# A two-branch attention kernel: another order of the first two groups, K of the first heads through two PSUM banks, and polynomial exponentials from group 1 on

## The chip, the cores and the metric

One Trainium2 chip, one core. The metric is device time in microseconds of one launch, the median of several runs. The engines named below are TensorE (PE, with its weight loads as PEld), VectorE (DVE), ScalarE (ACT), GpSimd (POOL) and SyncE (SP), which issues the DMAs.

## The reference

The input x has 2048 tokens of 640 features. Two attention branches with 32 heads of 20 features each are computed from the same x with weights of their own, and mixed by a gate for every token:

```python
qkv = (x @ wqkv).reshape(B, S, 3, 32, 20)
# A: full softmax attention over all 2048 keys
p = softmax(einsum("bhqd,bhkd->bhqk", q, k) * 20**-0.5);  a = (p @ v) @ wo
# B: each position attends to itself and 7 earlier ones, 2 apart
logits = einsum("bhsd,bhswd->bhsw", q, kg) * 20**-0.5;    b = (softmax(logits) @ vg) @ wo
g = sigmoid((x * gate_w).sum(-1))
out = g * a + (1 - g) * b
```

Branch A is by far the larger part: 32 heads x 2048 x 2048 exponentials.

## The kernel before, in words

**Tiling.** The heads of branch A are taken four at a time: `q` counts the eight quads of heads. One quad lies on the 128 partitions in four strips of 32, of which 21 are used (20 features, and one row that carries a shift, so that no maximum over the scores is needed). The queries are cut into four chunks `qc` of 512. A *group* is one quad with one query chunk, so there are 32 groups, numbered `g = qc * 8 + q`: all quads of the first chunk, then all of the second. A group has 16 key blocks of 128 keys times 4 heads = 64 *units*. One unit is a QK matmul of 128 keys x 512 queries, an exponential of 128 x 512, and a PV matmul.

**The main stream.** Units are gathered into *tiles* that use two PSUM areas in turn: `score[0]` with three banks (1536 columns) and `score[1]` with two (1024). For each tile, `qk` (L1090) issues its QK matmuls, `exp` (L1107) one ScalarE instruction over the whole tile into one of six `ebuf`s, and, two or more tiles later, `pv` (L1137) accumulates into the one bank `obank`. When a group's last PV is done, `close` adds `gen_norm`, which normalises and transposes the output into a slot of `oTn` on VectorE (L544 to L558).

**VectorE units ("rides").** In tiles of `score[0]` the third unit can be given to VectorE: the tile's exponential is then 1024 wide, and `gen_d` computes the third by a polynomial, in one step out of PSUM (L1101) and three more (L570, L573, L576). `wanted` decides where, once the planner's clock has passed `D0`, if VectorE is free enough. Whatever a VectorE unit does not take, ScalarE does.

**Everything else** runs beside that stream as generators with a priority number (the smaller, the sooner): `gen_k(q)` and `gen_q(g)` project K of a quad and Q of a group through one of the two `side` banks (the matmuls of all generators are recorded at L444), `gen_v(half)` projects V for four quads, `gen_gate` makes the gate of a chunk, `gen_bweights` reorders the weights of branch B on GpSimd (L590), `gen_bproj` and `gen_b` compute branch B, `gen_fold` and `gen_prefold` apply the output projections, and `tail` finishes the last chunk. A planner with costs of its own decides, at the time the program is written out, how these are interleaved in each engine's fixed order; TensorE runs strictly in that order. If the queries of the next group are not ready when its first tile comes, `run_until` puts all that is missing into the order at once. TensorE's gaps are filled with matmuls that compute nothing (`filler`, L1151 and L1155).

A new group starts its projections when the group ahead of it begins:

```python
if g1 + 1 < NQ:
    add_gen(gen_k(g1 + 1), 2)
add_gen(gen_q(g1 + 1), 2)
```

so each of the first eight groups needs a new K (four token chunks, 20 matmuls) as well as a Q.

**The start.** `turned(tcc)` transposes 512 tokens of x on TensorE into both score areas, ScalarE copies three fifths of the result (L917) and VectorE two fifths (L920). `k_first(tcc)` projects K of quad 0 for these tokens into `side[0]`; VectorE takes the largest magnitude of each row (L934), and after that ScalarE copies K to `kT` (L937). All four `tcc` use the same bank. `v_first` projects the first two V blocks, and Q of group 0 goes through `side[1]`.

Of the kernel before, what the change touches and what calls it, by code (L numbers as in the profile page):

```python
# [14 lines left out]
P = 128  # L15
# [3 lines left out]
DH = 20  # L19
# [10 lines left out]
TOK = 256  # L30

# [209 lines left out]
def _build(ctx, nc, A_x, A_wqkv, A_wo, B_wqkv, B_wo, gate_w, out):  # L241
# [114 lines left out]
    T("dve", 0.1, lambda e: e.memset(zero[:, :], 0.0), writes=["zero"])  # L356

    for i in range(7):
        T("pe", 0.43, lambda e: e.matmul(obank[:, :], qabs[:, 0:P], qabs[:, :], start=True, stop=True), reads=["qabs"], writes=["obank"])
# [120 lines left out]
    def gen_q(g):  # L480
        qc, q = divmod(g, NQ)
# [38 lines left out]
    def gen_gate(qc):  # L520
        while qc > 1 and not all(done.get(("norm", (qc - 2) * NQ + q)) for q in range(NQ)):
            yield ("cond",)
# [18 lines left out]
    def gen_norm(g):  # L541
        qc, q = divmod(g, NQ)
        sl = g % NSLOT
# [204 lines left out]
    def gen_prefold():  # L748
        while not (done.get(("b", 2 * QCN - 1)) and all(done.get(("norm", LQ + q)) for q in range(NQ - 1))):
            yield ("cond",)  # L750
# [61 lines left out]
    def gen_fold(qc):  # L812
        while not (done.get(("b", 2 * qc + 1)) and all(done.get(("norm", qc * NQ + q)) for q in range(NQ))):
            yield ("cond",)
# [99 lines left out]
    def turned(tcc):  # L914
        cols = slice(tcc * 512, (tcc + 1) * 512)
        turn(tcc, 0, 3, 0)
        T("act", actc(1536), lambda e: e.activation(  # L917
            xT[:, 0:3, cols], _ap(score[0], 0, [[512, 3], [1, 512]]), ACTF.Copy), reads=[("score", 0)], writes=[("xT", tcc, 0)])
        turn(tcc, 3, 5, 1)
        T("dve", dvc(1024), lambda e: e.tensor_copy(xT[:, 3:5, cols], _ap(score[1], 0, [[512, 2], [1, 512]])),  # L920
          reads=[("score", 1)], writes=[("xT", tcc, 1)])
# [7 lines left out]

    def k_first(tcc):  # L930
        cols = slice(tcc * 512, (tcc + 1) * 512)
        T("pe", 1.07, proj5(side[0][:, :], lambda c: kvw[:, WKP_OFF + c * NQ * P:WKP_OFF + c * NQ * P + P], None, tcc * 512),
          reads=[("WkP", 0)] + XT(tcc), writes=[("side", 0)])
        T("dve", dvc(512), lambda e: e.tensor_reduce(  # L934
            kmx4[:, tcc:tcc + 1], side[0][:, :], AX.X, ALU.max, apply_absolute_value=True),
          reads=[("side", 0)], writes=[("kmx4", tcc)])
        T("act", actc(512), lambda e: e.activation(kT[:, 0, cols], side[0][:, :], ACTF.Identity, bias=onesrow[:, 0:1]),  # L937
          reads=[("side", 0), "onesrow", ("kmx4", tcc)], writes=[("kT", 0, tcc)])

    def v_first(kb0, n, s_):  # L940
# [6 lines left out]
        T("pe", 0.67 * n, fn, reads=["WvA"] + XT(kb0 // 4) + XT((kb0 + n - 1) // 4), writes=[("score", s_)])  # L947
        for i in range(n):
            o = _ap(vA, (kb0 + i) * NQ * 4 * DV + 1, [[DV, 16], [1, DH]])
            i_ = _ap(score[s_], i * 512, [[DH, 16], [1, DH]])  # L950
            T("act", actc(320) + 0.1, lambda e, o=o, i_=i_: e.activation(o, i_, ACTF.Copy), reads=[("score", s_), "vAones"],
              writes=[("vA", kb0 + i, 0)])
            done[("v", kb0 + i, 0)] = True

    turned(0)
    T("dve", 0.36, w_pad(kvw, WKP_OFF, repB[0], 0, 4 * DH, 0), reads=["wk0", "WkP"], writes=[("WkP", 0)])
    T("dve", 0.36, w_pad(WqP, 0, repB[1], 0, 4 * DH, 0), reads=["wq0", "WqP"], writes=[("WqP", 0)])
    done[("pad", 0)] = True
    turned(1)
    k_first(0)  # L960
    T("pe", 1.07, proj5(side[1][:, :], lambda c: WqP[:, c, 0:P], None, 0), reads=[("WqP", 0)] + XT(0), writes=[("side", 1)])
    turned(2)
# [3 lines left out]
    k_first(1)  # L966
    turned(3)
    k_first(2)
    T("dve", 0.5, lambda e: e.memset(vA[:, :, :, :, 0:1], 1.0), writes=["vAones"])
    k_first(3)  # L970
    T("dve", 0.15, lambda e: e.tensor_reduce(kmx[:, 0:1], kmx4[:, :], AX.X, ALU.max),
# [3 lines left out]
    v_first(0, 2, 1)  # L975
    T("pe", 0.215, lambda e: e.matmul(side[1][:, :], KM[0][:, :], qabs[:, :], start=False, stop=True, skip_group_check=True),
      reads=[("KM", 0), "qabs"], accum=[("side", 1)])
    t = T("dve", dvc(512), lambda e: e.tensor_scalar(qT[0][:, :], side[1][:, :], OCT, offs[:, 0:1], op0=ALU.mult, op1=ALU.add),
# [21 lines left out]

    DTIME = 15.0
    DIDLE = -1.0
    D0 = 100.0
# [73 lines left out]
    def qk(s):  # L1077
# [8 lines left out]
        def fn(e):  # L1086
            ins = None
            for g, kb, j, o in lst:
                q = g % NQ
# [5 lines left out]
        for g, kb, j, _ in lst:  # L1095
            rd.add(("kT", g % NQ, kb // 4))
            rd.add(("qT", g % 2))
# [13 lines left out]
    def pv(units, quads):  # L1111
# [14 lines left out]
        for g, kb, j, _ in lst:  # L1126
            if not done.get(("v", kb, (g % NQ) // 4)):
                run_until(("v", kb, (g % NQ) // 4))
            rd.add(("vA", kb, (g % NQ) // 4))
# [4 lines left out]
        def fn(e):  # L1134
            ins = None
            for k, (g, kb, j, src) in enumerate(lst):
                ins = e.matmul(obank[32 * j:32 * j + DV, :], vA[:, kb, g % NQ, j, :], src,  # L1137
# [24 lines left out]
    def close(g):  # L1162
        nonlocal hold, obank_free
        if g >= NSLOT:
            run_until(("fold", (g - NSLOT) // NQ))
# [7 lines left out]
    obank_free = 0.0  # L1173
# [34 lines left out]
    while pvg < NG:  # L1208
# [11 lines left out]
        if acting:  # L1220
            gn = us[-1] // 64
            run_until(("q", gn))
            if gn != g1:
                g1 = gn

                if g1 + 1 < NG:
                    if g1 + 1 < NQ:
                        add_gen(gen_k(g1 + 1), 2)
                    add_gen(gen_q(g1 + 1), 2)
                if g1 == 1:  # L1230
                    add_gen(gen_v(1), 3)
                if g1 == 0:
                    add_gen(gen_gate(0), 3)
                if g1 == 2:
                    add_gen(gen_bweights(), 4)
                if g1 % NQ == 6 and g1 // NQ + 1 < QCN:
# [55 lines left out]
```

## Time and profile before

| | |
|---|---|
| time, three runs | 944.18, 946.05, 944.18 us; median 944.18 us |
| profiled run | 943.52 us, span of the profile 941.7 us, mean granted TensorE clock 0.992 |
| PE busy | 913.5 us, 97%, fillers included |
| ACT busy | 907.7 us, 96% |
| DVE busy | 684.1 us, 73% |
| POOL busy | 23.7 us, 3% |
| exponentials L1107 | 819 instructions, 891.7 us |

The span is one execution, from its first to its last instruction. A row of the timeline gives start and length of one instruction, or of several like ones that follow each other; the number of instructions is behind the x. The bracket at its end is the time that the engine stood idle ahead of it, and the instruction whose end released it. "Busy" of successive ScalarE instructions overlaps a little, so 819 exponentials at their mean length add up to more than the time that they fill.

### The profile page before, as it was taken

What the parts mean: (1) busy time and instruction counts of PE and PEld (TensorE: products, weight loads), DVE (VectorE), ACT (ScalarE), POOL (GpSimd) and SP (SyncE); (2) the same over time, 40 slices, a digit from 0 to 9 for tenths busy, and PEclk for the clock granted to TensorE, in tenths of its full rate; (3) what the DMA queues carried; (4) which work ended last, traced back from release to release, by engine and by line L of the source; (5) the groups of instructions that cost most, each with busy time, mean ns of one, the idle gap of its engine ahead of it and who ended that gap; (6) DMA issues with size and microseconds to landing.
All of it is one profiled execution on the core that took longest, in us unless ns stands there. A gap on an engine that the chain in (4) does not pass through costs nothing.

```text
span 941.7 us, 16802 instructions
## 1 busy us (share of the span) xinstructions
PE 913.5 (97%) x6827; PEld 313.6 (33%) x6827; DVE 684.1 (73%) x1174; ACT 907.7 (96%) x854; POOL 23.7 (3%) x20
## 2 busy tenths in 40 slices
PE   7989999998999999999999999999999999999997
PEld 4323322222333333333333333333433333343223
DVE  5655587778688878777687887688788565778872
ACT  5979999997999999999999999999999999999996
POOL 0000000009000000000000000000000000000000
PEclk9999999998999999999999999999999999999999
DMA  7110000020000000000000000000000000000000
GB/s 225 27 44 1 1 1 1 1 106 1 1 2 1 1 2 1 8 15 8 1 1 2 1 1 8 15 9 1 1 1 1 9 8 16 1 1 1 1 1 29
DMA packets 9769, 13.08 MB, mean 14 GB/s; under 512 B 2396, under 2 KB 8412, under 8 KB 9692
## 3 DMA queue, kind: packets, MB, share of 16 engines
q1 hardware_dynamic: 9692, 12.00, 3.9%
q8 instruction: 54, 0.88, 0.4%
q14 instruction: 23, 0.19, 0.1%
HBM read 9.38 MB, written 2.62 MB: 13 GB/s over the span
## 4 chain that ended last, share of the span: by engine, by line
ACT 42%; PE 41%; issue 12%; DVE 4%; DMA 0%; DVEq 0%; ACTq 0%
ACT ebuf L1107 41%; PE side L444 16%; PE score L1090 12%; PE obank L1137 7%; PE side L1151 2%; PE obank L1155 2%; DVE tD L570 1%; DVE gtan L1101 1%; PE side L926 1%; DMA oTn<-in_A_x_dram 0%; PE score L908 0%; ACT tB L694 0%; PE side L651 0%; DVE tD L573 0%; DVE eD L576 0%
## 5 line engine op out<-in xcount | busy, mean ns | idle before, releaser
L1107 ACT ACTIVATE ebuf<-score 128x1024 bf16<-128x1024 f32 (+1 forms) x819 | 891.7, 1303 | 13.6 <-PE score L1090 13.0
L1090 PE MATMUL score<-qT,kT 32*128 32x512 bf16 x2048 | 320.7, 385 | 10.3 <-ACT ebuf L1107 4.2
L1137 PE MATMUL obank<-ebuf,vA 128*21 128x512 bf16 x1953 | 179.8, 386 | 1.2 <-ACT ebuf L1107 1.2
L1090 PEld LDWEIGHTS score<-qT,kT 32*128 32x128 bf16 x2048 | 79.9, 91 | 251.7 <-ACT ebuf L1107 189.1
L444 PE MATMUL side<-xT,kvw 128*128 128x256 bf16 (+1 forms) x740 | 137.6, 297 | 0.0
L1101 DVE TENSOR_SCALAR gtan<-score 128x512 f32<-128x512 f32 x77 | 53.3, 692 | 72.0 <-PE score L1090 71.3
L1155 PE MATMUL obank<-xT,zero 128*128 128x512 bf16 x298 | 88.5, 383 | 0.0
L444 PEld LDWEIGHTS side<-xT,kvw 128*128 128x128 bf16 x740 | 58.7, 97 | 61.0 <-issue 46.6
L1137 PEld LDWEIGHTS obank<-ebuf,vA 128*21 128x21 bf16 x1953 | 41.4, 89 | 94.7 <-issue 88.4
L1151 PE MATMUL side<-xT,ident 128*128 128x512 bf16 x189 | 57.6, 384 | 0.0
L576 DVE SCALAR_TENSOR_TENSOR eD<-tD,gtan 128x512 int16<-128x512 f32 x77 | 54.4, 707 | 1.5
L570 DVE SCALAR_TENSOR_TENSOR tD<-gtan 128x512 f32<-128x512 uint16 x77 | 53.6, 696 | 2.2
L573 DVE SCALAR_TENSOR_TENSOR tD<-gtan,tD 128x512 f32<-128x512 uint16 x77 | 53.5, 694 | 1.6
L444 PE MATMUL side<-xT,WqP 128*128 128x512 bf16 x155 | 49.3, 393 | 5.3 <-DVE qB L624 4.5
L719 DVE TENSOR_TENSOR stage<-vB,repB 128x1280 bf16<-128x1280 bf16 x64 | 50.3, 821 | 1.0
L444 PE MATMUL side<-stage,ident 128*128 128x512 bf16 (+1 forms) x192 | 49.5, 348 | 0.0
L641 DVE TENSOR_TENSOR stage<-qB,kB 128x1280 bf16<-128x1280 bf16 x64 | 49.1, 820 | 0.3
L444 PE MATMUL side<-woA_r,oTn 128*128 128x512 bf16 (+1 forms) x248 | 49.3, 302 | 0.0
L1155 PEld LDWEIGHTS obank<-xT,zero 128*128 128x128 bf16 x298 | 24.0, 97 | 36.3 <-issue 25.1
L469 DVE TENSOR_SCALAR kT<-side,onesrow 128x512 bf16<-128x512 f32 x28 | 20.8, 744 | 19.8 <-PE side L444 19.5
L444 PE MATMUL side<-woBp,oB 128*128 128x512 bf16 (+1 forms) x160 | 33.3, 303 | 0.0
L544 DVE STREAM_TRANSPOSE oTt<-obank 128x512 f32<-128x512 f32 x32 | 22.8, 712 | 13.0 <-PE obank L1137 12.8
(126 smaller groups left out, 640.4 us busy)
## 6 DMA issues: line engine op xcount, KB each, us to landing
stage<-in_B_wqkv_dram SPq DMA_DIRECT2D x1, 2400.0 KB, 8.8
out_dram<-outsb SPq DMA_DIRECT2D x12, 160.0 KB, 1.8
stage<-in_A_wqkv_dram SPq DMA_DIRECT2D x1, 1600.0 KB, 11.7
oTn<-in_A_x_dram SPq DMA_DIRECT2D x2, 640.0 KB, 5.2
kvw<-in_A_wqkv_dram SPq DMA_DIRECT2D x1, 800.0 KB, 8.7
woA_r<-in_A_wo_dram SPq DMA_DIRECT2D x4, 200.0 KB
woBp<-in_B_wo_dram SPq DMA_DIRECT2D x5, 160.0 KB
oB<-in_A_x_dram SPq DMA_DIRECT2D x1, 640.0 KB, 7.0
```

Of the source, the lines that this page charges most:

```text
L444: ins = e.matmul(o, l, r, start=(first and i == 0), stop=(last and i == n - 1), skip_group_check=True)
L570: T("dve", dvc(512), lambda e: e.scalar_tensor_tensor(tD[:, :], nn, -OCT16, nn, op0=ALU.add, op1=ALU.mult), reads=[("xD", w)], writes=["tD"])
L573: T("dve", dvc(512), lambda e: e.scalar_tensor_tensor(tD[:, :], nn, H1, tD[:, :], op0=ALU.add, op1=ALU.mult), reads=[("xD", w), "tD"], wri ...
L576: T("dve", dvc(512), lambda e: e.scalar_tensor_tensor(eD[:, sl, :].bitcast(I16), tD[:, :], H2, xD[w][:, :], op0=ALU.mult, op1=ALU.add), re ...
L641: TB(dvc(CN * TOK, 2), lambda e, w=w, ks=ks: e.tensor_tensor(prodB(w), qB[:, :, :], ks, ALU.mult), reads=["qB", "kB"], writes=[("prod", w) ...
L719: TB(dvc(CN * TOK, 2), lambda e, w=w, vs=vs, rr=rr: e.tensor_tensor(prodB(w), vs, rr, ALU.mult), reads=["vB", ("repB", w4 % 2)], writes=[( ...
L1090: ins = e.matmul(o, kT[32 * j:32 * j + 32, q, kb * P:(kb + 1) * P], qT[g % 2][32 * j:32 * j + 32, :], start=True, stop=True)
L1101: T("dve", dvc(512), lambda e: e.tensor_scalar(xD[w][:, :], o, 128.0 * 127, 16384.0, op0=ALU.add, op1=ALU.max), reads=[("score", s % 2)], ...
L1107: exps[s] = T("act", actc(512 * n), lambda e: e.activation(ebuf[s % NE][:, 0:512 * n], score[s % 2][:, 0:512 * n], ACTF.Exp, scale=LN2 / 1 ...
L1137: ins = e.matmul(obank[32 * j:32 * j + DV, :], vA[:, kb, g % NQ, j, :], src, start=(kb == 0), stop=(last and k >= len(lst) - 4), skip_grou ...
L1151: t = T("pe", 0.215, lambda e, b=b: e.matmul(side[b][:, :], ident[:, :], xT[:, 0, 0:512], start=True, stop=True), reads=["ident", ("xT", 0 ...
L1155: T("pe", 0.215, lambda e: e.matmul(obank[:, :], zero[:, :], xT[:, 0, 0:512], start=False, stop=False, skip_group_check=True), reads=["zer ...
```

## The change

1. **Order of the groups.** A list `GROUPS` takes the place of `divmod(g, NQ)`. The first group is (chunk 0, quad 0), the second (chunk 1, quad 0), which uses the K that is already there. Then follow the other quads of chunk 0, those of chunk 1, and chunks 2 and 3 as before. `POS` maps back, for the conditions of the gates and folds. It is meant to give K of the second quad a whole group more time.
2. **The start.** K of quad 0 alternates between `side[0]` and `obank`. Its projection (`k_first`), maximum (`k_max`) and copy (`k_out`) are issued separately, so that copies of x and K can be ordered by hand; the copies of the V blocks (`v_out`) are separate as well. Padding of the first K and Q weights, and the ones in `vA`, move from VectorE to GpSimd. Two more warm-up matmuls stand ahead of the first transposes and four behind them.
3. **VectorE units from group 1 on.** `D0` goes from 100 to 50.
4. **Priorities.** Q gets 0.9, above V's 1; K stays at 2. The gates of chunks 0 and 1 both start at group 1.

```diff
+GROUPS = [(0, 0), (1, 0)] + [(0, q) for q in range(1, NQ)] + [(1, q) for q in range(1, NQ)] + [
+    (qc, q) for qc in range(2, QCN) for q in range(NQ)]
+POS = {c: g for g, c in enumerate(GROUPS)}
...
+    T("pool", 0.5, lambda e: e.memset(vA[:, :, :, :, 0:1], 1.0), writes=["vAones"])
...
-    for i in range(7):
-        T("pe", 0.43, lambda e: e.matmul(obank[:, :], qabs[:, 0:P], qabs[:, :], start=True, stop=True), reads=["qabs"], writes=["obank"])
+    for i in range(9):
+        T("pe", 0.43, warm_up, reads=["qabs"], writes=["obank"])
...
     def gen_q(g):
-        qc, q = divmod(g, NQ)
+        qc, q = GROUPS[g]
...
     def gen_norm(g):
-        qc, q = divmod(g, NQ)
-        sl = g % NSLOT
+        qc, q = GROUPS[g]
+        sl = (qc * NQ + q) % NSLOT
...
+    kbank = lambda tcc: (side[0], ("side", 0)) if tcc % 2 == 0 else (obank, "obank")
...
-    turned(0)
-    T("dve", 0.36, w_pad(kvw, WKP_OFF, repB[0], 0, 4 * DH, 0), reads=["wk0", "WkP"], writes=[("WkP", 0)])
-    T("dve", 0.36, w_pad(WqP, 0, repB[1], 0, 4 * DH, 0), reads=["wq0", "WqP"], writes=[("WqP", 0)])
+    turn(0, 0, 3, 0)
+    turn(0, 3, 5, 1)
+    for i in range(4):
+        T("pe", 0.215, warm_up, reads=["qabs"], writes=["obank"])
+    x_out(0)
+    T("pool", 0.8, w_pad(kvw, WKP_OFF, repB[0], 0, 4 * DH, 0), reads=["wk0", "WkP"], writes=[("WkP", 0)])
+    T("pool", 0.8, w_pad(WqP, 0, repB[1], 0, 4 * DH, 0), reads=["wq0", "WqP"], writes=[("WqP", 0)])
     done[("pad", 0)] = True
     turned(1)
     k_first(0)
+    turned(2)
+    k_max(0)
+    k_out(0)
     T("pe", 1.07, proj5(side[1][:, :], lambda c: WqP[:, c, 0:P], None, 0), reads=[("WqP", 0)] + XT(0), writes=[("side", 1)])
-    turned(2)
+    k_first(1)
+    turn(3, 0, 3, 0)
+    turn(3, 3, 5, 1)
+    k_max(1)
+    k_out(1)
+    x_out(3)
+    k_first(2)
...
+    k_max(2)
     k_first(3)
+    k_out(2)
+    v_first(0, 2, 1)
+    k_max(3)
...
-    D0 = 100.0
+    D0 = 50.0
...
-                        add_gen(gen_k(g1 + 1), 2)
-                    add_gen(gen_q(g1 + 1), 2)
+                        add_gen(gen_k(g1 + 1), KPRIO)
+                    add_gen(gen_q(g1 + 1), QPRIO)
                 if g1 == 1:
+                    add_gen(gen_gate(0), 1.5)
+                    add_gen(gen_gate(1), 1.6)
                     add_gen(gen_v(1), 3)
-                if g1 == 0:
-                    add_gen(gen_gate(0), 3)
...
-                if g1 % NQ == 6 and g1 // NQ + 1 < QCN:
+                if g1 in (14, 22):
                     add_gen(gen_gate(g1 // NQ + 1), 4)
```

In the excerpt KPRIO is 2.0 and QPRIO 0.9. Where `g % NQ` stood for the quad in `qk`, `pv` and `close`, `GROUPS[g]` stands now.

## The prediction

> **What bounds the kernel now.** I began with the page's busy times:
>
> ```profile
> PE 913.5 (97%) x6827; PEld 313.6 (33%) x6827; DVE 684.1 (73%) x1174; ACT 907.7 (96%) x854; POOL 23.7 (3%) x20
> ```
>
> TensorE and ScalarE are both nearly always busy. TensorE's figure is not a bound: 298 matmuls of L1155 and 189 of L1151 are fillers that compute nothing, about 487 x 0.22 us = 107 us (in the tail five matmuls of 512 columns take 1.24 us and seven 1.68, so one adds 0.22). ScalarE's work is real. So I took its instructions in order of time, from the first exponential to 300 us. The columns are start, length, engine, line, instruction, and in brackets the idle time ahead and what ended it:
>
> ```profile
> 24.41 1.45 ACT L1107 ACTIVATE ebuf<-score 128x1536 bf16<-128x1536 f32 x1 [0.78 <-PE score L1090]
> 26.40 27.23 ACT L1107 ACTIVATE ebuf<-score 128x1024 bf16<-128x1024 f32 x24 [0.55 <-PE score L1090]
> 58.16 3.28 ACT L1107 ACTIVATE ebuf<-score 128x1024 bf16<-128x1024 f32 x3 [4.54 <-PE score L1090]
> 62.60 2.37 ACT L1107 ACTIVATE ebuf<-score 128x1536 bf16<-128x1536 f32 x2 [1.16 <-PE score L1090]
> ...
> 235.07 1.02 ACT L1107 ACTIVATE ebuf<-score 128x1024 bf16<-128x1024 f32 x1 [5.43 <-PE score L1090]
> 236.64 31.32 ACT L1107 ACTIVATE ebuf<-score 128x1024 bf16<-128x1024 f32 x28 [0.55 <-PE score L1090]
> ```
>
> Once it has begun, ScalarE stops at only two places for long: 4.54 + 1.16 = 5.7 us near 58, and 5.43 + 0.55 = 6.0 us near 235. With 0.55 at the second exponential and 0.32 at 272.9, idle time is 12.6 us. The last exponential ends at 931.3 (a merged row: start 919.72, length 11.56). The span of 941.7 is thus 24.4 ahead of the first exponential, 906.9 between, 10.4 after. Of the 906.9, 894.3 is ScalarE working. The groups by shape price one unit of 512 columns:
>
> ```profile
> L1107 ACT ACTIVATE ebuf<-score 128x1024 bf16<-128x1024 f32 x504 | 536.7, 1139 | 11.6 <-PE score L1090 11.1 <-PE side L444 0.3 <-ACT ebuf L1107 0.2
> L1107 ACT ACTIVATE ebuf<-score 128x1536 bf16<-128x1536 f32 x315 | 493.0, 1565 | 2.0 <-PE score L1090 1.9
> ```
>
> 1565 - 1139 = 426 ns: what ScalarE saves when a tile gives its third unit to VectorE.
>
> The start, from the timeline of the first 32 us, shows the one-bank K chain, where each projection waits for ScalarE's copy of the previous one:
>
> ```profile
> 17.09 1.44 ACT L917 ACTIVATE xT<-score 128x1536 bf16<-128x1536 f32 x1
> 17.33 1.24 PE L926 MATMUL side<-xT,kvw 128*128 128x512 bf16 x5 [0.92 <-ACT kT L937]
> 18.61 0.69 DVE L934 TENSOR_REDUCE kmx<-side 128x1 f32<-128x512 f32 x1 [0.94 <-PE side L926]
> 19.39 0.69 ACT L937 ACTIVATE kT<-side,onesrow 128x512 bf16<-128x512 f32 x1 [0.87 <-DVE kmx L934]
> 20.22 1.24 PE L926 MATMUL side<-xT,kvw 128*128 128x512 bf16 x5 [1.65 <-ACT kT L937]
> ```
>
> Last, the stall near 235, from the timeline of 214 to 242 us:
>
> ```profile
> 213.10 24.08 POOL L590 COPY kvw<-stage 128x640 bf16<-128x640 bf16 x15 [212.04 <-DVE gtan L1101]
> ...
> 223.15 0.68 DVE L1101 TENSOR_SCALAR gtr<-score 128x512 f32<-128x512 f32 x1
> ...
> 226.73 1.70 DVE L570 SCALAR_TENSOR_TENSOR tD<-gtr 128x512 f32<-128x512 uint16 x1
> ...
> 228.47 1.69 DVE L573 SCALAR_TENSOR_TENSOR tD<-gtr,tD 128x512 f32<-128x512 uint16 x1
> 230.19 1.68 DVE L576 SCALAR_TENSOR_TENSOR eD<-tD,gtr 128x512 int16<-128x512 f32 x1
> 231.79 0.68 DVE L624 CAST qB<-side 128x512 bf16<-128x512 f32 x1
> ...
> 232.53 1.89 PE L444 MATMUL side<-xT,WqP 128*128 128x512 bf16 x4 [4.49 <-DVE qB L624]
> ```
>
> While GpSimd copies the weights of part B, VectorE's polynomial steps take up to 1.70 us instead of 0.70. The copy that frees TensorE's side bank stands behind them, and TensorE, which runs in order, waits 4.49 us with every later QK behind it.
>
> **What the Trainium skill says.** "ScalarE: Activation LUTs", section "What ACT_TABLE_LOAD costs": 0.833 ns an element, successive instructions overlapping; 512 columns are then 427 ns, and the 426 ns above agrees. "SBUF — State Buffer", section "Who interferes with whom": a VectorE instruction with two SBUF inputs contends with a GpSimd instruction that reads SBUF; one with a single SBUF input outside the two-port modes does not. The trace agrees: L570 to L576 go from 0.70 to 1.70 us beside copies of about 24.08 / 15 = 1.6 us, and the PSUM readers L1101 and L624 stay at 0.68. "TensorE: Matmul & The Clock Gate", section "What's actually happening": the array's clock halves when idle. Here it is 0.50 between 230 and 236 us, and 0.77 from 5 to 10 us.
>
> **The change part by part.**
>
> *Start.* Estimates from the durations above and the changed order. Two more fillers ahead and four behind the first transposes cover the gap in which the clock fell to 0.77. The second block's transposes still begin at 7.84, but at full clock their ScalarE copy starts near 8.65, not 9.32. The weight padding moves from VectorE (0.38 us each, twice) to GpSimd. Not seen there before; at GpSimd's 1.6 us for 640 elements it is 1.0 us for 400, bounds 0.7 to 1.8. It runs from the weights' landing at about 6.3 (issued 1.23, median 5.1 to landing) and ends before K needs it at 9.2, so it costs nothing. K then alternates side0 and obank. From 8.65 the ScalarE copies of x end at 10.1, 12.7 and 17.2 (the last behind two K copies); the last K projection starts at 17.2 instead of 20.22. From there to the first exponential was 4.19 us; fourth-K copy and V copies (0.69 + 0.76 us) fit beside the V projection and Q's bias. First exponential at 21.7: 2.7 us won. If the transposes stay slow, 1.8; at best 3.2.
>
> *Second group.* Group 1 becomes query chunk 1 of the same heads: K is ready, only Q is needed, and that is issued directly behind the first QK. In the changed order no tile is preceded by a lump of projections; before, eleven stood ahead of the tile at 57.7. The 4.54 and 1.16 go: 5.7 us. New: V's last blocks now come just in time, one block's five matmuls, its copy and the PV waiting for it between two QKs, for five or six pairs. One such pair costs TensorE about 0.8 + 0.75 + 0.4 + 0.7 = 2.65 us against ScalarE's 2.3; score's two banks hide part. Loss 0.7, bounds 0 to 1.5.
>
> *VectorE units.* The order holds 108 instead of 95 units, and 302 instead of 315 tiles of 1536. 13 x 0.426 = 5.5 us off ScalarE. Thirteen units are 13 x 4 x 0.70 = 36 us more on VectorE, which has 250 us free. Locally it is fuller: counting the ordered work by the mean durations of before, four stretches of 26 tiles come to 0.98 to 1.01 of ScalarE's time there. Before, the fullest was 1.03, with no idle of ScalarE around it, so I charge 1.0, bounds 0 to 5.
>
> *GpSimd's copies.* They start at nearly the same place (after tile 171). About three units, one output normalisation and a Q pass fall in their 24 us. Stepping through with 1.2 to 1.7 us for two-input steps, TensorE waits 1 to 2 us in each of three places (an eD for PV, the new qT for the filler behind it, an xD for the next QK), where it waited 4.5 in one before. Score's second bank hides about half. I take 3.0 for the old 6.0, bounds 1 and 10. Saved: 3.0.
>
> *Gates, priorities, bookkeeping.* Gates 0 and 1 move behind group 1's start, on TensorE instead of fillers; the fold of chunk 0 becomes possible one group later, far from where its slots are reused. Nothing.
>
> *End.* Behind the last exponential 24 fold matmuls remain where 20 or 21 did; TensorE ends last there, so 3 x 0.22 = 0.7 us more.
>
> Sum: first exponential 21.7; ScalarE 894.3 - 5.5 = 888.8; idle 0.55 + 0.3 + 0.7 + 1.0 + 3.0 = 5.6; tail 11.1. Span 927.2, 14.5 below 941.7. From 944.18, that is 929.7 us.
>
> **The rivals.** *A slow VectorE eats part of it.* For: it stands near 1.0 in four stretches, and three units meet GpSimd's copies. Against: TensorE's waits for units are only some 11 us, spread over 24. With 8 us around the copies and 1.3 more elsewhere: 929.7 + 5 + 1.3 = 936. *The stalls vanish altogether.* For: three short waits may hide behind score's second bank. Without 3.0 for the copies, 0.7 for V and 1.0 for the full stretches: 925. *Slower than before.* If TensorE, with no filler left in several stretches, meets late K or Q at boundaries, each stop costs what the one at 58 did, 5.7 us. Four full stretches stopping would be 929.7 + 22.8 = 952.5. Against: the order shows no forced lump, and regions as full ran without idle before.
>
> **How the numbers follow.** Forecast 0.55; slow VectorE 0.24; stalls gone 0.15; slower 0.04; rest 0.02 near no change. The time is the forecast's, 929.7. The range, 923.5 to 938, goes from the second rival with the best start (925 - 0.5, and a little) to the first with the copies at their bound of 10 us and a poor start. Faster 0.94, same 0.02, slower 0.04.
>
> **What would show it.** First exponential near 21.7; no ScalarE idle near 50 to 63; 302 tiles of 1536 at 1565 ns; around GpSimd's copies ScalarE idle near 3 us in pieces; elsewhere under 2. It is wrong if ScalarE's waits for QK exceed 12 us in total, if the exponentials themselves grow longer, or if stops appear where V or units are waited for.

## The result, and the profile after

The changed kernel took 930.79 us (median of four runs: 930.41, 937.86, 930.40, 931.18), the kernel before 944.98 (944.17 to 946.05, four runs); the ratio is 0.9867, 95% interval 0.9818 to 0.9915. The span of the profile fell from 941.7 to 928.6 us. The run of 937.86 had a mean TensorE clock of 0.991 where the profiled one had 0.997; it has no trace of its own, but `few_warm_ups` below, whose order behind the start is the same, shows what such a difference can be.

The page's busy times after:

```profile
PE 882.1 (95%) x6677; PEld 309.4 (33%) x6785; DVE 718.1 (77%) x1223; ACT 902.8 (97%) x854; POOL 26.0 (3%) x23
```

VectorE has 34 us more work and ScalarE 4.9 less. TensorE shows 31 us less, but most of that is not work saved: 108 matmul records are missing from this trace (6677 matmuls beside 6785 weight loads), about 108 x 0.22 = 24 us. Counted by their weight loads, the fillers went from 487 to 439, which is an estimated 48 x 0.22 = 11 us. The groups by shape show the trade, 13 exponentials moved from 1536 to 1024 columns:

```profile
L1146 ACT ACTIVATE ebuf<-score 128x1024 bf16<-128x1024 f32 x517 | 543.2, 1128 | 6.6 <-PE score L1129 6.0
L1146 ACT ACTIVATE ebuf<-score 128x1536 bf16<-128x1536 f32 x302 | 469.1, 1553 | 1.3 <-PE score L1129 1.3
```

ScalarE in order of time, from the first exponential on, every place where it stood idle (columns as before: start, length, engine, line, instruction, and in brackets the idle time ahead and what ended it):

```profile
21.00 1.45 ACT L1146 ACTIVATE ebuf<-score 128x1536 bf16<-128x1536 f32 x1 [0.72 <-PE score L1129]
23.04 22.70 ACT L1146 ACTIVATE ebuf<-score 128x1024 bf16<-128x1024 f32 x20 [0.59 <-PE score L1129]
46.37 4.66 ACT L1146 ACTIVATE ebuf<-score 128x1024 bf16<-128x1024 f32 x4 [0.62 <-PE score L1129]
51.23 4.37 ACT L1146 ACTIVATE ebuf<-score 128x1024 bf16<-128x1024 f32 x4 [0.20 <-PE score L1129]
56.18 5.12 ACT L1146 ACTIVATE ebuf<-score 128x1024 bf16<-128x1024 f32 x5 [0.58 <-PE score L1129]
...
218.49 1.02 ACT L1146 ACTIVATE ebuf<-score 128x1024 bf16<-128x1024 f32 x1 [0.75 <-PE score L1129]
219.79 1.02 ACT L1146 ACTIVATE ebuf<-score 128x1024 bf16<-128x1024 f32 x1 [0.27 <-PE score L1129]
220.97 4.62 ACT L1146 ACTIVATE ebuf<-score 128x1024 bf16<-128x1024 f32 x4 [0.15 <-PE score L1129]
227.07 1.02 ACT L1146 ACTIVATE ebuf<-score 128x1024 bf16<-128x1024 f32 x1 [1.49 <-PE score L1129]
229.02 1.02 ACT L1146 ACTIVATE ebuf<-score 128x1024 bf16<-128x1024 f32 x1 [0.92 <-PE score L1129]
230.48 5.12 ACT L1146 ACTIVATE ebuf<-score 128x1024 bf16<-128x1024 f32 x5 [0.44 <-PE score L1129]
236.19 33.82 ACT L1146 ACTIVATE ebuf<-score 128x1536 bf16<-128x1536 f32 x31 [0.59 <-PE score L1129]
```

The stop of 4.54 + 1.16 us near 58 is gone. In its place stand three short waits, 0.62 + 0.20 + 0.58 = 1.4 us. Beside GpSimd's copies there are 0.75 + 0.27 + 0.15 + 1.49 + 0.92 + 0.44 + 0.59 = 4.6 us. From 236 us to the last exponential (its end: 917.3) there is no wait at all. The span adds up as follows, in us:

| part of the span | before | after |
|---|---|---|
| to the first exponential | 24.4 | 21.0 |
| ScalarE working, first to last exponential | 894.3 | 889.7 |
| its waits | 12.6 | 6.6 |
| behind the last exponential | 10.4 | 11.3 |
| sum | 941.7 | 928.6 |

The waits from 46 to 57 are the V blocks that now come just in time. The timeline of 44 to 47 us shows one of them:

```profile
44.79 0.49 DVE L519 CAST vA<-side 128x320 bf16<-128x320 f32 x1 [1.05 <-PE side L451]
...
45.34 0.61 PE L1176 MATMUL obank<-ebuf,vA 128*21 128x512 bf16 x8 [0.58 <-DVE vA L519]
...
45.88 0.60 PE L1129 MATMUL score<-qT,kT 32*128 32x512 bf16 x5
```

PV waits 0.58 us for the cast of its V block, QK stands behind PV in TensorE's order, and ScalarE stands idle for 0.62 us until QK is done (the row at 46.37 above).

The waits from 217 to 236 are read from the timeline of that stretch:

```profile
209.29 23.02 POOL L597 COPY kvw<-stage 128x640 bf16<-128x640 bf16 x15 [200.51 <-PE side L451]
...
213.97 1.71 DVE L580 SCALAR_TENSOR_TENSOR tD<-gtan,tD 128x512 f32<-128x512 uint16 x1
...
215.71 1.69 DVE L583 SCALAR_TENSOR_TENSOR eD<-tD,gtan 128x512 int16<-128x512 f32 x1
...
217.46 0.40 PE L1176 MATMUL obank<-ebuf,vA 128*21 128x512 bf16 x4 [1.43 <-DVE eD L583]
...
226.08 0.39 PE L451 MATMUL side<-qabs,KM 128*128 128x512 bf16 x1 [1.91 <-DVE qabs L499]
...
228.30 0.61 PE L1129 MATMUL score<-qT,kT 32*128 32x512 bf16 x3
...
235.69 0.39 PE L1129 MATMUL score<-qT,kT 32*128 32x512 bf16 x3 [0.89 <-DVE gtan L1140]
```

A polynomial step that takes 0.69 us elsewhere takes 1.7 here. Ahead of the `qabs` that ends the second wait, two steps of an output normalisation (L556 and L562) take 1.35 and 1.88 us; in `short_pool` below, without the long copies, they take 0.17 and 0.69. TensorE waits for VectorE in three places. Between the last two, a QK of three matmuls takes 0.61 us where the others take 0.39, and the windows show that TensorE's granted clock fell (it is the figure 0.59; from 226.7 to 230.1 us alone it was 0.50):

```profile
core 0: us, PE busy (x) PEld busy (x) DVE busy (x) ACT busy (x) POOL busy (x), PEclk, DMA share, GB/s
...
226.00:230.00 4.00, 3.92 (x18) 0.90 (x18) 2.92 (x6) 2.01 (x2) 3.88 (x3) 0.59 0.00 0
```

So the wait of 1.91 us at 226 is followed by 1.49 + 0.92 + 0.44 = 2.85 us of ScalarE's waits, more than the wait itself.

### The profile page after: what moved, and what is told of

Read it like the earlier page. It is cut to its first block, busy times and chain, and to the rows that moved or that the text cites. A ratio compares the mean times of both kernels' runs of the same rounds, so it can differ in the third digit from the quotient of the medians.

```text
span 928.6 us, 16664 instructions
## 1 busy us (share of the span) xinstructions
PE 882.1 (95%) x6677; PEld 309.4 (33%) x6785; DVE 718.1 (77%) x1223; ACT 902.8 (97%) x854; POOL 26.0 (3%) x23
## 4 chain that ended last, share of the span: by engine, by line
ACT 61%; issue 18%; PE 16%; DVE 3%; DMA 1%; DVEq 0%; ACTq 0%
ACT ebuf L1146 60%; PE side L451 6%; PE score L1129 5%; PE obank L1176 3%; PE obank L1194 1%; DVE eD L583 1%; DVE tD L580 1%; DMA oTn<-in_A_x_dram 1%; DVE gtan L1140 0%; ACT tB L701 0%; PE score L915 0%; DVE tD L577 0%; ACT xT L928 0%; DVE vA L519 0%; PE side L658 0%
## 5 line engine op out<-in xcount | busy, mean ns | idle before, releaser
L1140 DVE TENSOR_SCALAR gtan<-score 128x512 f32<-128x512 f32 x90 | 62.2, 691 | 82.1 <-PE score L1129 81.8
L1194 PE MATMUL obank<-xT,zero 128*128 128x512 bf16 x268 | 80.2, 384 | 2.1 <-issue 1.6
L583 DVE SCALAR_TENSOR_TENSOR eD<-tD,gtan 128x512 int16<-128x512 f32 x90 | 64.1, 712 | 2.2
L580 DVE SCALAR_TENSOR_TENSOR tD<-gtan,tD 128x512 f32<-128x512 uint16 x90 | 63.8, 709 | 1.9
L577 DVE SCALAR_TENSOR_TENSOR tD<-gtan 128x512 f32<-128x512 uint16 x90 | 62.6, 695 | 2.6
L451 PE MATMUL side<-woA_r,oTn 128*128 128x128 bf16 (+1 forms) x242 | 47.4, 300 | 0.2 <-issue 0.2
L451 PE MATMUL side<-xT,WqP 128*128 128x512 bf16 x139 | 43.0, 384 | 0.7 <-issue 0.7
L1190 PE MATMUL side<-xT,ident 128*128 128x512 bf16 x122 | 37.6, 385 | 0.7 <-issue 0.5
L451 PE MATMUL side<-woBp,oB 128*128 128x128 bf16 (+1 forms) x152 | 31.5, 298 | 0.6 <-issue 0.5
L451 PE MATMUL side<-kvw,xT 128*128 128x320 bf16 x150 | 30.3, 302 | 0.5 <-DVE tD L580 0.2
```

The source lines that it names most:

```text
L451: ins = e.matmul(o, l, r, start=(first and i == 0), stop=(last and i == n - 1), skip_group_check=True)
L577: T("dve", dvc(512), lambda e: e.scalar_tensor_tensor(tD[:, :], nn, -OCT16, nn, op0=ALU.add, op1=ALU.mult), reads=[("xD", w)], writes=["tD"])
L580: T("dve", dvc(512), lambda e: e.scalar_tensor_tensor(tD[:, :], nn, H1, tD[:, :], op0=ALU.add, op1=ALU.mult), reads=[("xD", w), "tD"], wri ...
L583: T("dve", dvc(512), lambda e: e.scalar_tensor_tensor(eD[:, sl, :].bitcast(I16), tD[:, :], H2, xD[w][:, :], op0=ALU.mult, op1=ALU.add), re ...
L1140: T("dve", dvc(512), lambda e: e.tensor_scalar(xD[w][:, :], o, 128.0 * 127, 16384.0, op0=ALU.add, op1=ALU.max), reads=[("score", s % 2)], ...
L1190: t = T("pe", 0.215, lambda e, b=b: e.matmul(side[b][:, :], ident[:, :], xT[:, 0, 0:512], start=True, stop=True), reads=["ident", ("xT", 0 ...
```

## The experiments

Every kernel below was timed beside the kernel before, whose medians in these sessions were 945.4 to 946.3 us. Where a result is compared with another one, ratios to before are given, since sessions ran on different chips.

### The parts alone

**The new start alone:** the kernel after with the old order, gates and priorities, and D0 at 100.

```diff
-GROUPS = [(0, 0), (1, 0)] + [(0, q) for q in range(1, NQ)] + ...
+GROUPS = [(g // NQ, g % NQ) for g in range(QCN * NQ)]
-    QPRIO = 0.9
+    QPRIO = 2
-    D0 = 50.0
+    D0 = 100.0
...
-                    add_gen(gen_gate(0), 1.5)
-                    add_gen(gen_gate(1), 1.6)
...
+                if g1 == 0:
+                    add_gen(gen_gate(0), 3)
...
-                if g1 in (14, 22):
+                if g1 % NQ == 6 and g1 // NQ + 1 < QCN:
```

> The new start alone, on the old order of groups, old gates and priorities, D0 of 100; 95 VectorE units, as before. Ledger (each part of the change earns its own time on ScalarE's line, and the parts add up): first exponential at 21.0 instead of 24.4 us, stall near 58 and stall beside GpSimd's copies still there, so 944.98 - 3.4 = 941.6 us. Rival (TensorE's load of V, K and Q in the first group sets when group 1 can begin, so an earlier start is given back at the stop near 58): that stop grows from 5.7 to about 9 us, and the time stays at 945.

Measured: 940.66 us (939.84 to 942.67), ratio 0.9945 (0.9926 to 0.9964). The start was not given back at the stop near 58. The gain by the ratio is 5.2 us (3.4 to 7.0) where the sum said 3.4, so the sum lies at the edge of the interval. ScalarE's timeline has the early first exponential, the stop that belongs to the old order, and the old stall beside the copies:

```profile
20.95 1.45 ACT L1145 ACTIVATE ebuf<-score 128x1536 bf16<-128x1536 f32 x1 [0.72 <-PE score L1128]
...
54.71 3.28 ACT L1145 ACTIVATE ebuf<-score 128x1024 bf16<-128x1024 f32 x3 [4.54 <-PE score L1128]
...
231.57 1.02 ACT L1145 ACTIVATE ebuf<-score 128x1024 bf16<-128x1024 f32 x1 [5.42 <-PE score L1128]
```

The profiled run is the longest of the four (942.67 us); beside the copies it has 8.1 us of waits in all, where the trace of before has 6.0.

**The new order alone:** before's start, the new `GROUPS`, gates and priorities, D0 at 100.

```diff
+GROUPS = [(0, 0), (1, 0)] + [(0, q) for q in range(1, NQ)] + ...
...
-        qc, q = divmod(g, NQ)
+        qc, q = GROUPS[g]
...
+                    add_gen(gen_gate(0), 1.5)
+                    add_gen(gen_gate(1), 1.6)
```

> The new order of groups with its gates and priorities, old start, D0 of 100; 101 VectorE units in the order. Ledger: the stop of 5.7 us near 58 goes, waits for V of about 1.4 us come, six units more are worth 6 x 0.43 = 2.6 us: 944.98 - 6.9 = 938.1 us, give or take 3 for what the units beside GpSimd's copies do. Rival (the stop near 58 is TensorE's load in the first two groups, not the wait for K, and returns one group later): 942 to 943.

Measured: 937.74 us (936.65 to 944.15), ratio 0.9938 (0.9915 to 0.9961). The stop near 58 is gone in this kernel too, and only waits of 0.62 and 0.20 us stand there; the order removes it, without the new start.

```profile
51.02 4.66 ACT L1115 ACTIVATE ebuf<-score 128x1024 bf16<-128x1024 f32 x4 [0.62 <-PE score L1098]
55.88 4.80 ACT L1115 ACTIVATE ebuf<-score 128x1024 bf16<-128x1024 f32 x4 [0.20 <-PE score L1098]
```

The profiled run is one of the long ones (943.76 us). Beside the copies and behind them ScalarE waits 10.0 us there, in part while TensorE's clock is at 0.50 (241.6 to 258.6 us).

**D0 = 50 alone**, in the kernel before.

```diff
-    D0 = 100.0
+    D0 = 50.0
```

> D0 of 50 alone in the kernel before; the order holds 94 VectorE units, one fewer than before, only placed earlier. Ledger (what counts is how many units ScalarE is spared): +0.4, no change beyond 1 us, 944 to 946. Rival (earlier units pay by themselves, because the first groups are ScalarE's slowest): under 943.

Measured: 949.17 us (948.71 to 950.65), ratio 1.0040 (1.0024 to 1.0056): slower, which neither theory had. The planner placed 94 units where before has 95, the stop of 4.54 us is still there, and new ones come near 352, 2.6 us in all. By the traces the waits beside the copies are also 1.2 us longer than in before, and the time behind the last exponential 1.7 us:

```profile
59.16 5.54 ACT L1107 ACTIVATE ebuf<-score 128x1024 bf16<-128x1024 f32 x5 [4.54 <-PE score L1090]
...
352.73 2.37 ACT L1107 ACTIVATE ebuf<-score 128x1024 bf16<-128x1024 f32 x2 [1.07 <-PE score L1090]
```

**D0 = 100 in the kernel after.**

```diff
-    D0 = 50.0
+    D0 = 100.0
```

> The changed kernel with D0 back at 100; the order holds 99 VectorE units instead of 108. Ledger: 9 units more on ScalarE, 9 x 0.43 = 3.9 us, first exponential at 21.0 still: 930.8 + 3.9 = 934.7, give or take 3 for the stall beside GpSimd's copies. Rival (VectorE is so full with 108 units that what ScalarE is spared comes back as waits): 929 to 931.5.

Measured: 941.24 us median, with a spread from 936.03 to 948.01 over 20 runs; ratio 0.9952 (0.9930 to 0.9973). Its order holds 99 units where after has 108, and 9 x 0.426 = 3.8 us on 930.8 are 934.6: only the fastest runs come near that. The sum misses the spread. A run's time follows its mean TensorE clock: about 936 us at 0.996, 941 to 942 at 0.989, 948 at 0.980. TensorE's timeline of the profiled run (936.81 us) shows one such place:

```profile
620.09 0.39 PE L1129 MATMUL score<-qT,kT 32*128 32x512 bf16 x3 [1.18 <-ACT ebuf L1146]
621.69 1.04 PE L1176 MATMUL obank<-ebuf,vA 128*21 128x512 bf16 x8 [1.21 <-DVE oTt L551]
622.66 1.03 PE L1129 MATMUL score<-qT,kT 32*128 32x512 bf16 x5
```

After two waits of 1.2 us five QK matmuls take 1.03 us, not 0.60.

So the 13 more units are not D0's alone: the order by itself gives 101, the start 95, D0 in the old kernel 94, all together 108. A planner's parts do not add up. Their times don't either: the fastest run of late_d0, 936.0 us, is hardly better than the fastest of the order alone, 936.7, though the start is some 3 us earlier. Each kernel is a new interleaving, and what the parts have in common is read from the places in the trace, not from differences of totals.

### What the copies cost

**Copies cut to one element.** GpSimd's 15 weight copies are still issued, but each moves a single element, so that branch B's weights are not reordered; one memset on GpSimd at the start fills the rest. The order of the other engines is that of after.

```diff
-                T("pool", 2.2, lambda e, o=o, i=i: e.tensor_copy(o, i), reads=["stage"],
+                T("pool", 2.2, lambda e, o=o, i=i: e.tensor_copy(o[:, 0:1, 0:1, 0:1], i[:, 0:1, 0:1, 0:1]), reads=["stage"],
...
+    T("pool", 0.8, lambda e: e.memset(kvw[:, WV_OFF + CN * D:3 * CN * D], 0.0), writes=["kvw_rest"])
```

> The changed kernel with each of GpSimd's 15 weight copies cut to one element in each partition, at the same place in the order, so branch B's weights are not reordered and its part of the output is not computed from the right weights. All other engines keep their order: 108 VectorE units. Port theory (VectorE's two-input steps wait for GpSimd's reads of SBUF): these steps stay at 0.7 us between 205 and 240, ScalarE's idle there falls from 4.6 us to under 1, and the time to 930.8 - 4 = 926.8 us. Rival (VectorE has too much to do there: three units, an output normalisation, a Q pass): idle of 3 us or more stays, 929.5 to 931.

Measured: 925.36 us (925.01 to 925.55), ratio 0.9788 (0.9774 to 0.9803). ScalarE's idle times go straight from the last V wait to the tail:

```profile
56.81 5.12 ACT L1147 ACTIVATE ebuf<-score 128x1024 bf16<-128x1024 f32 x5 [0.58 <-PE score L1130]
...
918.87 1.08 ACT L808 ACTIVATE stage<-side 128x512 bf16<-128x512 f32 x2 [6.42 <-PE side L789]
```

All of the waits that after has from 217 to 236 go with the length of the copies: the order of TensorE, VectorE and ScalarE is the same in both. Together with them went the spread: four runs within 0.6 us, all at a clock of 0.999 or 1.000.

**No unit begun beside the copies.** The copies are planned at 1.5 us, and `wanted` says no while they run.

```diff
+            if now < bw_end[0]:
+                return None
```

> The changed kernel in which no VectorE unit is begun while GpSimd's weight copies run (and these copies are planned at 1.5 us, nearer to what they take, instead of 2.2); 105 units. Port theory: without the units' two-input steps only the normalisation and the KM step meet the copies; ScalarE's idle there falls from 4.6 to 1.5 us or less, 3 units fewer cost 1.3: about 929 us. Rival (the stall is not made by the units' steps): idle there stays at 4 us or more and the time rises to 932.

Measured: 936.09 us (935.66 to 939.21), ratio 0.9909 (0.9889 to 0.9930). Beside the copies the waits fell to 0.74 + 0.28 us, as expected; the time did not. The planner's order changed behind them, with 105 units and stops that after does not have, 7.7 us in all, the longest at 342:

```profile
219.59 28.73 ACT L1151 ACTIVATE ebuf<-score 128x1536 bf16<-128x1536 f32 x25 [0.28 <-PE score L1134]
...
341.95 2.37 ACT L1151 ACTIVATE ebuf<-score 128x1024 bf16<-128x1024 f32 x2 [3.45 <-PE score L1134]
```

**No VectorE units at all.**

```diff
-    D0 = 50.0
+    D0 = 1e9
```

> The changed kernel without any VectorE unit: ScalarE computes all exponentials, 410 tiles of 1536 and 409 of 1024. Ledger: 108 x 0.426 = 46.0 us more ScalarE work, less about 3 us of idle beside GpSimd's copies: 973 to 977 us. Rival (a unit given to VectorE saves less than its columns, because small gaps come with it): 0.35 a unit, 969 or less.

Measured: 972.49 us (two runs, 969.50 and 975.47), ratio 1.0287 (1.0245 to 1.0330). Beside the copies only 0.31 us of waiting is left. By the ratios, (1.0287 - 0.9867) x 945 / 108 = 0.37 us is what a unit brings net in this kernel; it takes 0.426 off ScalarE, and the copies take back 4.3 / 108 = 0.04 of that. The 0.02 that are left fit the time behind the last exponential, 9.0 us here and 11.3 in after. The 15 copies took 20.73 us here and 23.02 in after: GpSimd is held up by VectorE as well.

**Shorter copies.** If the long steps are waits for one copy each, a short copy should hold them up less. Each copy is split into five of 128 elements; the order on TensorE, VectorE and ScalarE is exactly that of after.

```diff
-                o = _ap(kvw, (m * CN + c) * D, [[P, CN], [32, 4], [1, 32]])
-                i = _ap(stage, c * 3 * D + m * D, [[1, CN], [CN, 4], [DH, 32]])
+                for f in range(CN):
+                    o = _ap(kvw, (m * CN + c) * D + f * P, [[32, 4], [1, 32]])
+                    i = _ap(stage, c * 3 * D + m * D + f, [[CN, 4], [DH, 32]])
```

> The kernel after with each of GpSimd's 15 weight copies (640 elements a partition, 1.5 us) split into five of 128 elements; the order of TensorE, VectorE and ScalarE stays what it is. Theory A (a VectorE step with two operands in SBUF waits for the GpSimd copy that is under way, and so for at most the rest of one copy): the two-input steps beside the copies take about 1.0 us instead of 1.7, ScalarE's waits from 209 to 240 us fall from 4.6 to about 1.5, and the time is 927 to 928. Theory B (the two engines share the port by time, so the whole time of the copies counts): the waits stay at 4.6 or grow, as 75 copies carry 75 fixed costs, and the time is 930 to 933.

Measured: 933.04 us (932.50 to 933.48), ratio 0.9858 (0.9839 to 0.9877). Theory A was right about the step and wrong about the time; theory B named nearly the right time, though the steps contradict its reason, sharing by time: ScalarE's waits from 209 us on grew to 7.0 us, and the trace shows why. From the timelines of 205 to 262 us:

```profile
209.33 41.17 POOL L598 COPY kvw<-stage 128x128 bf16<-128x128 bf16 x75 [200.67 <-PE side L451]
...
213.59 0.78 DVE L580 SCALAR_TENSOR_TENSOR tD<-gtan,tD 128x512 f32<-128x512 uint16 x1
...
222.41 1.16 PE L451 MATMUL side<-xT,kvw 128*128 128x256 bf16 x9 [1.28 <-POOL kvw L598]
...
238.49 0.61 PE L451 MATMUL side<-xT,kvw 128*128 128x256 bf16 x2 [3.85 <-POOL kvw L598]
...
239.03 0.61 PE L1130 MATMUL score<-qT,kT 32*128 32x512 bf16 x2
```

The two-input step takes 0.78 us, nearly its undisturbed 0.69. But 75 copies take 41.17 us instead of 23.02, and TensorE now waits for GpSimd itself, 1.28 us for the weights of q and 3.85 for those of k; behind the latter the clock is halved again (two matmuls in 0.61). A wait for the other engine's instruction was traded for a wait for its data.

**Copies split as far as their readers allow.** q's copies in two, k's in three, v's in five.

```diff
-                for f in range(CN):
+                for f, n in ((0, 3), (3, 2)) if m == 0 else ((0, 2), (2, 2), (4, 1)) if m == 1 else [(f, 1) for f in range(CN)]:
```

> GpSimd's weight copies split only as far as their readers leave time: q's in two (384 and 256 elements a partition), k's in three (256, 256, 128), v's in five of 128; the order of TensorE, VectorE and ScalarE stays that of after. From 1.535 us a copy of 640 elements and 0.549 us one of 128, a copy of n elements takes 0.302 us + 1.926 ns x n, so that q's weights are there at 218.5 us (the projection asks at 221.1), k's at 229.2 (asked at 234.6) and v's at 242.9. Theory A (a short copy cannot hold up a two-input step, and split_copies lost only through weights that came late): no wait of TensorE for GpSimd, two-input steps of about 1.1 us beside q's copies and 0.8 us beside v's, ScalarE's waits from 209 us on 1 to 2 us, and 926 to 928.5 us. Theory B (whatever is spared in the steps is given back by the longer stretch in which the two engines share the port): the waits stay at 4 us or more and the time is 930 to 933.

Measured: 926.01 us (925.42 to 933.39, six runs), ratio 0.9818 (0.9788 to 0.9847). In the timelines of this kernel:

```profile
208.94 35.09 POOL L598 COPY kvw<-stage 128x384 bf16<-128x384 bf16 x50 [200.48 <-PE side L451]
...
214.69 1.24 DVE L583 SCALAR_TENSOR_TENSOR eD<-tD,gtan 128x512 int16<-128x512 f32 x1
...
226.34 0.78 DVE L583 SCALAR_TENSOR_TENSOR eD<-tD,gtan 128x512 int16<-128x512 f32 x1
```

And ScalarE's waits in its whole timeline behind the V waits:

```profile
219.50 11.53 ACT L1147 ACTIVATE ebuf<-score 128x1024 bf16<-128x1024 f32 x11 [0.15 <-PE score L1130]
231.18 33.82 ACT L1147 ACTIVATE ebuf<-score 128x1536 bf16<-128x1536 f32 x31 [0.15 <-PE score L1130]
```

Steps grow with the length of the copies beside them: 1.7 us at 640 elements, 1.0 to 1.25 at 384 and 256, 0.78 to 1.0 at 256 and 128, 0.78 at 128. No matmul waits longer than 0.44 us for VectorE there, and ScalarE's 4.6 us have become 0.3. By its median this is the fastest kernel with the full computation, and it lies 0.7 us above the copies of one element, in another session. Its interval and that of after overlap (0.9788 to 0.9847 and 0.9818 to 0.9915), so that the gain in time over after, 0.5% by the ratios, rests on the traces more than on the times. Two of its six runs (930.63 and 933.39) had clocks of 0.992 and 0.989, the other four 1.000; the two have no trace.

### The waits for V

K of the second quad is held back until V is complete.

```diff
+        while q == 1 and not done.get(("v", KBN - 1, 0)):
+            yield ("cond",)
```

> The changed kernel in which K of the second quad begins only when V of the first four quads is complete, so that V has both side banks; 103 units. Theory (the three waits of 0.6, 0.2 and 0.6 us near 46, 51 and 56 come from V's serial use of one bank while K holds the other): these waits, 1.4 us, go; 5 units fewer cost 2.1: about 931.5 us, with ScalarE idle under 0.3 us from 24 to 60. Rival (TensorE's load is the limit and the waits move to the boundary of group 2, near 80): idle of 1.4 us or more shows later.

Measured: 936.58 us (932.75 to 939.99), ratio 0.9898 (0.9859 to 0.9937). The three waits did disappear: no wait from 23 to 217 us. But the order holds 103 units, not 108, and in the profiled run the stall beside the copies ended in a long stretch at half clock. The windows of that kernel give busy time by engine, and then the granted clock:

```profile
core 0: us, PE busy (x) PEld busy (x) DVE busy (x) ACT busy (x) POOL busy (x), PEclk, DMA share, GB/s
...
228.00:253.00 25.00, 25.00 (x118) 6.98 (x116) 14.23 (x19) 16.25 (x15) 3.33 (x2) 0.50 0.00 1
```

TensorE is busy for all of the 25 us, at 0.50, and ScalarE for 16.25: TensorE is the bound there. So the 1.4 us of V waits come from K being worked on beside V; whether it is the bank or the engines' time that K takes from V, this run does not separate. It was not a way to get them back.

### The start

**One bank for K**, with the copies of x and V ordered as in after; the third K is copied ahead of the fourth projection, which now needs its bank. Only the start is read.

```diff
-    kbank = lambda tcc: (side[0], ("side", 0)) if tcc % 2 == 0 else (obank, "obank")
+    kbank = lambda tcc: (side[0], ("side", 0)) if True else (obank, "obank")
...
+    k_out(2)
     k_first(3)
-    k_out(2)
```

> The kernel after with K of the first heads through one bank again (the first side bank), the last projection of the order put back behind the third K; the copies stay off ScalarE's chain. Theory A (the second bank is what shortened the start): each projection waits for the copy of the one before it, and the first exponential starts at about 24 us instead of 21.0. Theory B (it was the order and the warm clock, and the bank is idle luck): it starts at 21.0 to 21.7. Only the start is read.

The first exponential starts at 24.64 us (one run, 938.90 us). The second K projection waits for the first one's way out of the bank:

```profile
11.78 1.24 PE L936 MATMUL side<-xT,WqP 128*128 128x512 bf16 x5
14.67 1.24 PE L936 MATMUL side<-xT,kvw 128*128 128x512 bf16 x5 [1.65 <-ACT kT L957]
```

In after it ran at 12.65, without a wait.

**Fewer warm-up products**: seven instead of nine, and none behind the first transposes.

```diff
-    for i in range(9):
+    for i in range(7):
...
-    for i in range(4):
-        T("pe", 0.215, warm_up, reads=["qabs"], writes=["obank"])
```

> The kernel after with seven warm-up products instead of nine and without the four behind the first transposes. Theory A (the 0.7 us by which the start was better than forecast came from TensorE's full clock): the granted clock is below 1.00 between 5 and 10 us, and the first exponential starts at 21.7 to 21.9 instead of 21.0. Theory B (the warm-ups change nothing, and x landed as it did): clock and start stay, 21.0. Only the start is read, counted from the first transpose, as the landing of x varies by 0.2 us.

The first exponential starts at 22.38 us (one run, 936.93 us); x landed 0.35 us later in this run, so 1.0 us is the warm-ups'. Twenty transposes take 2.29 us, not 1.28, and the windows show the clock at 0.76:

```profile
8.35 2.29 PE L915 MATMUL score<-ident,oTn 128*128 128x128 bf16 x20 [1.19 <-ACT xT L928]
```

```profile
core 0: us, PE busy (x) PEld busy (x) DVE busy (x) ACT busy (x) POOL busy (x), PEclk, DMA share, GB/s
...
5.00:10.00 5.00, 2.94 (x36) 2.80 (x37) 1.44 (x4) 1.62 (x2) 1.04 (x2) 0.76 1.10 343
```

Counted from the first transpose to the first exponential: before 24.41 - 5.37 = 19.0 us, after 21.00 - 5.52 = 15.5, with one bank 24.64 - 5.34 = 19.3, with few warm-ups 22.38 - 5.87 = 16.5. Of the 19.3 some 0.4 is x, which came in while the first transposes ran (they took 1.68 us instead of 1.29). Without the second bank the warm-ups and the freed copies bring next to nothing.

Behind the start, the kernel with few warm-ups has the order of after on TensorE, VectorE and ScalarE, instruction by instruction. Its profiled run had a mean clock of 0.991, and so shows how this order can run long:

```profile
228.35 7.24 ACT L1144 ACTIVATE ebuf<-score 128x1024 bf16<-128x1024 f32 x7 [1.39 <-PE score L1127]
237.40 2.43 ACT L1144 ACTIVATE ebuf<-score 128x1536 bf16<-128x1536 f32 x2 [1.81 <-PE score L1127]
```

TensorE waits for VectorE in the same three places, here for 1.43, 1.89 and 1.89 us. Its clock is at 1.00 until 236.3 us, and up to there and through the third wait ScalarE loses 1.18 + 1.39 + 1.81 = 4.4 us. Then TensorE runs at half clock until 249.9 us, and ScalarE waits for another 4.4 us.

## Why the prediction was right, point by point

The time was forecast at 929.7 us and came out at 930.8; the span was forecast at 927.2 and came out at 928.6. Most of the mechanism is shown by the runs above. Of its signs of being wrong, waits for V and for units did appear, but where the forecast itself had them (1.4 and 4.6 us against 0.7 and 3.0). The near hit is partly luck, as errors of both signs cancelled: -0.7 + 0.7 - 0.3 - 1.0 + 1.6 for the steps below, 0.9 more of ScalarE's own time, and 0.2 in the tail.

- *Start*, forecast 21.7, measured 21.00. The mechanism is shown: the second bank is necessary, and the warm-ups keep the clock at 1.00. The size was a little off: the warm-ups were worth 1.0 us and not the 0.67 by which one copy starts earlier, and the last K projection began at 16.80 rather than 17.2. From there it is 4.20 us to the first exponential, against 4.19 in before; the forecast's own terms, 17.2 + 4.19, give 21.4 and not 21.7, so that 0.3 of the difference is in its sum. The bound for slow transposes, 1.8 us won, was too low: with few warm-ups 19.0 - 16.5 = 2.5 are won.
- *Weight padding on GpSimd*, forecast 1.0 us each: 0.52 and 0.53, and hidden.
- *Second group*: the 5.7 us near 58 went, and order_only shows that the order does it. The new V waits were forecast at 0.7 (bounds 0 to 1.5) and measured at 1.4, by the mechanism that was named: cast, PV, QK, ScalarE. So less was hidden by the second score bank than assumed; no run separates that from the size of the waits. The 0.3 us at 272.9, which the forecast kept, went as well.
- *VectorE units*: 108 and 302 as in the order. The pace agrees with the 426 ns: by the median, the next exponential starts 904 or 905 ns after one of 1024 columns and 1330 or 1331 after one of 1536, in every kernel but no_rides (911 and 1347). 13 x 0.426 = 5.5 us went, but ScalarE's work fell by 4.6. Its other instructions don't account for the rest: they fill 6.4 to 6.5 us in both traces. An estimate that is large enough is lost overlap: exponentials of 1024 columns last 1.02 us and start 0.90 apart, so each gap also costs the 0.12 by which they overlap, and the trace of after has 21 gaps, the shortest included, where before has 11: 10 x 0.12 = 1.2 us for the 0.9 that are missing. No run tests it.
- *Full stretches of VectorE*, charged with 1.0: nothing. There is no wait from 236 us on.
- *GpSimd's copies*, forecast 3.0, measured 4.6. The three waits of TensorE are the three that were named, an eD for PV, Q (its qabs, ahead of qT) and an xD for the next QK, with 1.43, 1.91 and 0.89 us, in the 1 to 2 us given but for the last. What failed is the sentence "Score's second bank hides about half": the waits of TensorE sum to 4.2 and ScalarE's to 4.6. Around the first and the third wait a fifth to a third was hidden (1.17 of 1.43 and 0.59 of 0.89 reached ScalarE); behind the second, TensorE was at half clock for 3.4 us and 1.91 became 2.85. But the clock is not why the sum was too low. In few_warm_ups it stayed at 1.00 there, 1.39 of 1.89 reached ScalarE, the third wait was longer instead (1.81 of 1.89 reached ScalarE), and the three sum to 4.4, about as much. So the bank hid about a fifth or less, not half. That the copies are the root of it all is shown by short_pool.
- *Tail*: forecast +0.7, measured +0.9; TensorE has 23 fold matmuls behind the last exponential in this trace, and 20 in before.

Of the rivals, "slow VectorE" was too dear: beside the copies VectorE cost 4.6 us and not 8, and its full stretches elsewhere cost nothing instead of 1.3. "The stalls vanish", at 925, is what short_pool (925.4) and graded_copies (926.0) reached once the copies no longer disturbed. "Slower than before" named stops at late K or Q; after has none, though other interleavings (d0_only, no_rides_beside) do have new stops.

On the section "Who interferes with whom" of "SBUF — State Buffer" in the Trainium skill: it says that the engine that comes first holds the shared ports for its whole instruction and the other one is blocked meanwhile. The ports themselves are seen in no trace; what the runs show agrees: the step's delay falls from 1.0 to 0.1 us when the copy beside it shrinks from 640 to 128 elements, at the same amount of data.

## What to carry to other kernels

When one engine's instruction can block another's, cut the blocking instruction shorter, but only as far as the readers of its data leave time: the fivefold split mended every blocked step and lost it again through late data. Price a wait of TensorE by what comes after it as well: waits of 1.2 to 1.9 us were followed by half clock for 3.4 us (after) to 27 us (k_after_v), though not always (the wait of 1.89 us at 227 in few_warm_ups was not). Where a planner writes out the order, judge an edit by the places in the trace that it was meant for; the total also holds the planner's other choices, which in d0_only and no_rides_beside outweighed the edit.

## What was not expected of the hardware

- **Half clock after short waits.** Where the granted clock fell in the midst of work, it was 0.50: from 226.7 to 230.1 us in after, 236.3 to 249.9 in few_warm_ups, 226.0 to 253.3 in k_after_v, 621.5 to 628.3 in late_d0, and behind the wait of 3.9 us in split_copies. In the 3.4 us ahead of the first four of these stretches TensorE had been busy for 1.2 to 1.9 us, with waits of 1.2 to 1.9 us between. In such a stretch TensorE, not ScalarE, can set the pace, as it does in k_after_v, and ScalarE waits again and again. The same order can get a short stretch or a long one: after ran at half clock for 3.4 us behind the second wait beside the copies, few_warm_ups for 13.6 us from the third on, with nearly the same first two waits. late_d0 spreads over 12 us, with the mean clock between 0.980 and 0.996, while short_pool, where nothing waits beside the copies, spreads over 0.6. "TensorE: Matmul & The Clock Gate", section "What's actually happening", in the Trainium skill gives about 3.4 us as the window over which idleness is judged; here two waits of 1.2 us with 0.4 us of work between them were enough. That the long runs without a trace are ones with such a stretch is inferred from their clock.
- **A memset on GpSimd that blocks a cast.** In after the ones of `vA` are set on GpSimd in 2.37 us, where VectorE had taken 0.48. A cast on VectorE with one operand in SBUF (L358), begun 0.09 us later, took 2.35 us instead of 0.23. It takes 2.35 us in the traces of start_only, late_d0 and no_rides too, which have the memset there, and 0.23 in those of before, order_only and d0_only, which don't. The identity matrix was ready at 3.7 us instead of 1.6; the first transposes waited for x until 5.5 in any case, so that it cost nothing here.
